# Softmax attention and hedgehog attention on one core: zero matmuls in more places, score pairs repeated, a start without DMA transposes

## The chip, the core and the metric

The kernel runs on one core of a Trainium2 chip. The core has five engines with a queue of instructions each: PE (TensorE, matmuls; PEld in the profile is its weight load), DVE (VectorE), ACT (ScalarE), POOL (GpSimd) and SP (SyncE, which here only issues DMAs). PE writes its results to PSUM, which has eight banks of 128 partitions by 512 floats; DVE and ACT read them there. An engine works through its own queue in order, and semaphores hold an instruction back until another engine or a DMA has done what it needs. The metric is the time on the device in microseconds (us).

PE's array can be used whole (128 rows by 128 columns), as four row tiles (32 rows each, four small contractions side by side) or as four column tiles (four narrow outputs side by side). The profile shows beside every stretch which share of its full clock PE was granted ("PEclk", 1.00 or 0.50 at any one moment).

## What is computed

Two layers of attention over 2048 tokens of width 512, with 32 heads of width 16, in bfloat16; their outputs are put side by side.

```
A:  q, k, v = split(x @ wqkv)
    p = softmax(q @ k.T * 16**-0.5)          # per head, 2048 x 2048
    out_A = (p @ v) @ wo
B:  q, k, v = split(x @ wqkv)
    phi(t) = concat(softmax(t @ w_phi), softmax(-(t @ w_phi)))
    kv = phi(k).T @ v ;  z = sum(phi(k))     # per head, 32 x 16
    out_B = (phi(q) @ kv / (phi(q) @ z + 1e-6)) @ wo
out = concat(out_A, out_B)
```

Layer A is nearly all of the work: 32 x 2048 x 2048 scores, each needed once for the row maximum and once for the exponential.

## The kernel before

**The plan.** The program isn't written in the order in which it runs. While it is built, a planner in Python steps through an imagined time. Every operation is a node with an engine, what it depends on, a booked duration and a priority; at each step `try_eng` (ACT, DVE, POOL, SP) or `try_pe` (PE) picks what starts next. The order that comes out is written into the engines' queues, and the chip keeps that order whatever its own times are. Bookings are simple sums: a 512-column matmul 0.213 us, an activation columns / 1200 + 0.067, a DVE instruction columns / 960 + 0.07.

**Layer A by units.** A unit is four heads (one head group of eight; each head lies on 32 partitions of its own) by 512 queries. There are 8 x 4 of them; the first and the last are cut into four of 128 queries, which makes 38. For a unit:

1. `try_m1_of` (L758): scores, queries by keys, one 32-row tile and 512 keys each. Two go to two neighbouring banks, and one DVE instruction (L766) takes both maxima. 1024 such pairs make up nearly all of DVE's work. A pair is split into two single ones where no two banks are free (it never was in this program).
2. `row_max` (L787 to L804): DVE joins the partial maxima; POOL splits the negated maximum into two bfloat16 halves; SP transposes them by DMA and puts them in two spare rows of the unit's queries. The keys have ones there, so the next product has the maximum subtracted already.
3. `try_m2` (L831): scores again, keys by queries, one row tile per bank; ACT takes the exponential into a ring of 16 slots (L327, pT). 2048 such blocks make up nearly all of ACT's work.
4. `try_pv` (L888): four column tiles multiply the exponentials with the values; bank VB = 7 gathers a unit's 16 key blocks. The values have a column of ones, which gives the sum.
5. `normalise` (L924 to L938): ACT copies the bank out (X); DMAs, ACT and POOL multiply by the reciprocal sum; then the output projection follows as a job.

The first step runs ahead of the third; the distance is called the lead here, in units of 512 queries.

**Jobs.** All whole-array work is put in jobs with a bank of their own: the projections of A (L433 for queries and keys, L472 for values), of B (L522, L536, L582), B's small products (L590, L616) and the output projections (L632, L645). A job is cut into pieces; a piece starts when `hurts` says that DVE will not be made to wait by more than a limit (JL), which grows with the job's delay. A job's piece is booked at 0.43 us. Evacuations of jobs are ACT's.

**Layer B** is released tile by tile (`fm`, every 31.5 us of planned time) and runs between the units: DVE L547 and L549, the wide work on POOL and ACT. Its denominator is inverted on ACT as a logarithm and an exponential (den_t).

**Zero matmuls.** `try_fill` comes last in `try_pe`. A list, `area`, holds how much of the array was planned busy in the last 3.4 us. While that is under FILL = 0.46 of it, and `hurts` allows it, a matmul with zeros as moving operand is put in, which adds nothing to what it accumulates on. In row mode with a unit open in bank 7 it is one row tile (L1048); in column mode, four column tiles of 17 columns (L1059); with no unit open, a full one to a free bank (L1069). Between the units, in row mode, there is none.

**The start.** ACT's queue loads the three weight blocks of A (L403). SP's queue loads x with DMA transposes, four for every 512 tokens (L409). The first projections wait for the first four.

Of the kernel before, what the change touches and what calls it, by code (L numbers as in the profile page):

```python
# [95 lines left out]
class _Node:  # L96
    __slots__ = ("eng", "run", "deps", "occ", "lat", "prio", "at", "seq", "tok", "start", "done", "frees", "ready",
                 "after")

    def __init__(self, eng, run, deps, occ, lat, prio, at, seq):  # L100
        self.eng = eng
        self.run = run
        self.deps = deps
        self.occ = occ
        self.lat = lat
        self.prio = prio
        self.at = at
        self.seq = seq
        self.tok = None
        self.start = None  # L110
        self.done = None
        self.frees = ()
        self.ready = None
        self.after = None

# [24 lines left out]
def bass_concat_heads__softmax_full_mha__linear_kernel_hedgehog__prompt_kernel(  # L140
# [23 lines left out]
    with contextlib.ExitStack() as es:  # L164
# [20 lines left out]
        eps_t = sb("eps_t", [128, 1], F32)  # L185
# [19 lines left out]
        W3 = sb("W3", [128, 4, 16], BF)  # L205
        hmask = sb("hmask", [128, 8], F32)
# [118 lines left out]
        def act(out_, in_, func, cols, reads=(), writes=(), deps=(), prio=5, sbuf=False, at=0.0, **kw):  # L325
            c = cols / 1200.0
            return mk("act", lambda ds: P.op("act", lambda e: e.activation(out_(), in_(), func, **kw), ds),  # L327
                      reads, writes, deps, occ=c + (0.093 if sbuf else 0.067) + (0.093 if "bias" in kw else 0.0),
                      lat=c + (0.28 if sbuf else 0.26) + (0.093 if "bias" in kw else 0.0), prio=prio, at=at)
# [13 lines left out]

        jobs = []
# [14 lines left out]
        def quads(fn, n=4, size=2):  # L359
# [30 lines left out]
        pool(lambda e: e.memset(eps_t[:], 1e-6), 0.1, (), ["eps"], prio=5)  # L390
# [11 lines left out]
        for i in range(3):  # L402
            dma("wa%d" % i, lambda e, i=i: e.dma_start(  # L403
                wA[:, :, i * 512:(i + 1) * 512], wa_v[:, :, i * 512:(i + 1) * 512]), (), [("wA", i)], prio=0,
                us=0.5, land=5.5 + i, q="act")

        def load_xa(c):
            for ct in range(4):
                dma("xa%d" % c, lambda e, ct=ct: e.dma_start_transpose(  # L409
                    xAT[:, ct, c * 512:(c + 1) * 512], A_x[0][c * 512:(c + 1) * 512, ct * 128:(ct + 1) * 128]),  # L410
                    (), [("xA", c, ct)], prio=0.5 + 0.1 * c if c else 0, us=1.29, land=3.6)

        for c in range(NC):
            load_xa(c)

# [12 lines left out]
        def proj_kq(kind, G, c, want, direct):  # L428
# [6 lines left out]
                want, [("wA", 0 if kind == "q" else 1)] + [("xA", c, ct) for ct in range(4)])  # L435
# [43 lines left out]

        proj_kq("k", 0, 0, 0, True)  # L480
# [39 lines left out]
        for x in (1, 0):  # L520
            for ct in range(4):
# [3 lines left out]
                    [("wT", i) for i in range(8)] + [("BD", t) for t in range(4)])  # L525
# [63 lines left out]
        def kv_job(burst, hf, want):  # L589
# [5 lines left out]
                [("phi", k) for k in range(4)] + [("vB", k) for k in range(4)], projs)  # L595
# [14 lines left out]
        def q_side(st, want):  # L610
# [4 lines left out]
            for hf in range(2):  # L615
# [3 lines left out]
                    [("phiT", i), ("kvd", hf)])  # L619
# [40 lines left out]
        m1_of = {}  # L660
        m2 = {"u": 0, "b": 0, "n": 0, "left": []}
# [67 lines left out]
        def try_m1_of(u, sm, single):  # L729
# [13 lines left out]
            if half is not None or not pair_free() or held["m"] > 2:  # L743
# [26 lines left out]
            r1_nodes.setdefault(u, []).append(d)  # L770
            if not sm["left"] and sm["half"] is None:
# [39 lines left out]
        def try_m2():  # L811
# [7 lines left out]
            if nfree() < 1 or held["e"] >= (EMAX - 1 if held["g"] or job_ready(now) else EMAX):  # L819
# [180 lines left out]
        def try_job():  # L1000
# [6 lines left out]
            if j is None:  # L1007
                if held["g"] >= 1 or (nfree() < 1):
# [25 lines left out]

        def try_fill():
            now = state["now"]
            while area and area[0][0] < now - 3.4:
                area.pop(0)
            if "end" in state or not vz[0]:
                return False  # L1040
            low = now < 9.0 or sum(a for _, a in area) < FILL * 3.4
            if not low:
                return False
            if state["mode"] == "row" and pv["open"]:
                for r in range(4):
                    old = state["fillrow"]
                    if prow[r] <= now + 1e-6 and (old is None or old[0] == r or done_by(old[1], now)):
                        n = pe_op([lambda e, r=r: e.matmul(  # L1048
                            PS[:, VB, :], ones_t[32 * r:32 * r + 32, :], zmv[32 * r:32 * r + 32, :], start=False,
                            stop=False, tile_position=(32 * r, 0), skip_group_check=True)],  # L1050
                            [t_zmv, t_ones] + ([old[1]] if old is not None and old[0] != r else []), "row", (r,))
# [4 lines left out]
            if pv["open"]:  # L1056
                if state["mode"] == "full" or not pe_ok("col", slack=0.0):
                    return False
                pe_op([lambda e, q=q: e.matmul(  # L1059
                    PS[32 * q:32 * q + 17, VB, :], ones_t[:, 0:17], zmv[:, :], start=False, stop=False,  # L1060
                    tile_position=(0, 32 * q)) for q in range(4)], [t_zmv, t_ones], "col")
            else:
                if not pe_ok("full", slack=0.0):
                    return False
                ok = [b for b, t in bank_free.items() if t is not None and t <= now + 1e-6]
                if not ok:
                    return False
                b = ok[-1]
                pe_op([lambda e: e.matmul(PS[:, b, :], ones_t[:, :], zmv[:, :], start=True, stop=True)],  # L1069
# [196 lines left out]
```

## Time and profile before

| | |
|---|---|
| three runs | 1660.59, 1691.67, 1699.48 us; median 1691.67 |
| the profiled execution | 1687.07 us, its span 1685.3 us |
| granted PE clock, mean | 0.69 |
| DVE | 1243.9 us busy, of it L766 1202.2 us (1024 instructions) |
| ACT | 1247.1 us busy, of it exponentials 1106.8 us (2048) |
| PE | 1605.2 us busy (10027 matmuls in the trace), of it zero matmuls L1048 860.6 us |
| POOL | 368.5 us busy |
| first and last score reduce | start at 18.9 and 1577.4 us |

Durations of matmuls that run side by side on several tiles overlap; a line's busy time is the time in which at least one runs that is put down to it. A row of a group reads: line, engine, operation, what it writes and reads, shapes, count; busy us and mean ns of one; idle time of the engine ahead of them and what ended it. Counts of a program's order, used below, are of the instructions as they stand in the queues, which hold no time.

### The profile page before, as it was taken

To read this page: it belongs to the slowest core of one execution; us is meant where nothing else is said; L and a number is where in the kernel's file an instruction comes from. 1 tells how busy PE (TensorE), PEld (TensorE's weight loads), DVE (VectorE), ACT (ScalarE), POOL (GpSimd) and SP (SyncE) were. 2 spreads that over 40 slices of the span, in tenths; PEclk is the share of its full clock that TensorE was granted. 3 is DMA by queue.
4 is the path that set the end of the run, shared out by engine and by line. 5 is a ranking of instruction groups with operands and counts; after the bars stand their busy time and mean duration, and the time that the engine had idled before them with its cause. 6 is when DMAs were issued, how large, how long until landed. Compare 5 with 4: busy or idle time off the path is not lost.

```text
span 1685.3 us, 24949 instructions
## 1 busy us (share of the span) xinstructions
PE 1605.2 (95%) x10027; PEld 471.6 (28%) x10085; DVE 1243.9 (74%) x1129; ACT 1247.1 (74%) x2475; POOL 368.5 (22%) x502
## 2 busy tenths in 40 slices
PE   5888999999999999999999999999999999999998
PEld 1332332222222322222222222222222222222234
DVE  5999996888799976798888666667788666666300
ACT  2887986788778966788778666667777666666666
POOL 2193731322222321132222122122210000000000
PEclk9997995777688955588777555556668555555557
DMA  5201000000001001111111011001100000000000
GB/s 114 55 5 40 5 6 5 5 6 5 4 15 9 5 1 18 18 24 18 21 30 21 11 17 15 14 11 18 24 16 22 5 4 5 4 3 7 6 4 17
DMA packets 70509, 26.71 MB, mean 16 GB/s; under 512 B 60728, under 2 KB 68472, under 8 KB 70392
## 3 DMA queue, kind: packets, MB, share of 16 engines
q1 hardware_dynamic: 68664, 23.47, 9.7%
q10 hardware_dynamic: 1728, 1.64, 0.3%
q8 instruction: 79, 1.29, 0.3%
q14 instruction: 38, 0.31, 0.1%
HBM read 3.16 MB, written 4.19 MB: 4 GB/s over the span
## 4 chain that ended last, share of the span: by engine, by line
PE 66%; DVE 19%; ACT 10%; POOL 3%; issue 1%; DMA 1%; SPq 0%; ACTq 0%; DVEq 0%; POOLq 0%
PE PS L1048 22%; DVE part L766 17%; PE PS L831 17%; PE PS L758 10%; PE PS L888 10%; ACT pT L327 8%; PE PS L536 2%; POOL QT L463 2%; PE PS L645 2%; PE PS L632 1%; PE PS L433 1%; PE PS L472 1%; DVE mB L547 1%; DVE mB L549 1%; ACT KT L327 0%
## 5 line engine op out<-in xcount | busy, mean ns | idle before, releaser
L766 DVE TENSOR_REDUCE part<-PS 128x2 f32<-128x1024 f32 x1024 | 1202.2, 1219 | 315.8 <-PE PS L1048 134.0
L327 ACT ACTIVATE pT<-PS 128x512 bf16<-128x512 f32 x2048 | 1106.8, 626 | 322.5 <-PE PS L831 153.1
L1048 PE MATMUL PS<-zmv,ones_t 32*128 32x512 bf16 x2176 | 860.6, 522 | 0.3
L831 PE MATMUL PS<-QT,KT 32*128 32x512 bf16 (+1 forms) x2432 | 769.0, 456 | 13.8 <-ACT pT L327 4.7
L758 PE MATMUL PS<-KT,QT 32*128 32x512 bf16 x2048 | 613.2, 500 | 20.0 <-DVE part L766 17.9
L1048 PEld LDWEIGHTS PS<-zmv,ones_t 32*128 32x128 bf16 x2176 | 223.1, 114 | 227.9 <-issue 187.2
L831 PEld LDWEIGHTS PS<-QT,KT 32*128 32x128 bf16 x2432 | 176.8, 100 | 369.6 <-ACT pT L327 236.0
L888 PE MATMUL PS<-pT,VP 128*17 128x512 bf16 (+1 forms) x2432 | 262.8, 452 | 0.4
L758 PEld LDWEIGHTS PS<-KT,QT 32*128 32x128 bf16 x2048 | 116.5, 99 | 174.5 <-DVE part L766 104.2
L888 PEld LDWEIGHTS PS<-pT,VP 128*17 128x17 bf16 x2432 | 55.4, 91 | 278.1 <-issue 265.8
L551 POOL TENSOR_TENSOR uB<-pB,mB 128x512 f32<-128x512 f32 x32 | 33.8, 1057 | 378.9 <-DVE mB L547 342.5
L938 POOL TENSOR_TENSOR QT<-X,Yd 128x256 bf16<-128x256 f32 (+1 forms) x67 | 45.5, 696 | 244.9 <-ACT pT L327 88.6
L796 POOL TENSOR_SCALAR stage<-mrow 128x16 bf16<-128x16 f32 (+1 forms) x38 | 9.3, 246 | 365.1 <-DVE mrow L787 365.1
L568 POOL TENSOR_TENSOR wA<-eB,rB 128x1024 bf16<-128x1024 bf16 x32 | 61.7, 1927 | 72.1 <-ACT rB L327 65.6
L976 DVE TENSOR_TENSOR QT<-PS,Yd 128x128 bf16<-128x128 f32 x1 | 0.3, 293 | 100.5 <-ACT Yd L327 100.5
L433 PE MATMUL PS<-xAT,wA 128*128 128x512 bf16 x118 | 33.8, 396 | 21.1 <-DMA xAT<-in_A_x_dram 9.8
L536 PE MATMUL PS<-Wf,xBT 128*128 128x512 bf16 x115 | 47.8, 525 | 4.2 <-issue 2.5
L557 POOL TENSOR_TENSOR sB<-eB 128x512 f32<-128x512 bf16 x32 | 36.9, 1153 | 49.9 <-ACT eB L327 49.9
L626 POOL TENSOR_TENSOR oB<-yB,den_t 128x512 bf16<-128x512 f32 x16 | 16.9, 1054 | 125.6 <-ACT den_t L327 125.6
L463 POOL TENSOR_SCALAR QT<-SG,kmask 128x512 bf16<-128x512 bf16 x28 | 43.2, 1562 | 0.6 <-ACT SG L327 0.6
L645 PE MATMUL PS<-WOp,QT 128*128 128x512 bf16 x113 | 36.0, 443 | 2.8 <-issue 1.2
L560 POOL TENSOR_TENSOR sB<-sB 128x256 f32<-128x256 f32 x64 | 36.0, 562 | 4.2
(83 smaller groups left out, 520.2 us busy)
## 6 DMA issues: line engine op xcount, KB each, us to landing
Yd<-Yd SPq DMA_DIRECT2D x120, 32.0 KB, 3.2
out_dram<-xAT SPq DMA_DIRECT2D x16, 128.0 KB, 1.7
out_dram<-OA SPq DMA_DIRECT2D x15, 128.0 KB, 1.7
wA<-in_A_wqkv_dram ACTq DMA_DIRECT2D x3, 512.0 KB, 5.8
QT<-mcols SPq DMA_DIRECT2D x60, 4.0 KB
mcols<-stage SPq DMA_TRANSPOSE x38, 2.3
WOp<-in_A_wo_dram SPq DMA_DIRECT2D x8, 64.0 KB, 3.1
woB<-in_B_wo_dram SPq DMA_DIRECT2D x1, 512.0 KB, 3.8
```

The source lines that it names most:

```text
L327: return mk("act", lambda ds: P.op("act", lambda e: e.activation(out_(), in_(), func, **kw), ds), reads, writes, deps, occ=c + (0.093 if s ...
L433: j = job(quads(lambda e, b, ct: e.matmul(PS[:, b, :], wA[:, ct, col:col + 128], xAT[:, ct, sl], start=(ct == 0), stop=(ct == 3))), want, ...
L463: kq_nodes[(kind, g, c)] = pool(lambda e, g=g, gl=gl: e.tensor_scalar(T[:, g, sl], SG[:, k, :], kmask[:, gl:gl + 1], None, ALU.mult), 0.7, ...
L536: j = job(quads(lambda e, b, ct: e.matmul(PS[:, b, :], xBT[:, ct, st * 128:(st + 1) * 128], Wf[:, x, ct, :], start=(ct == 0), stop=(ct == ...
L568: pool(lambda e: e.tensor_tensor(phiB[k].rearrange("p (g f) -> p g f", f=16), e3, rB[:, i, :].unsqueeze(2).broadcast_to([128, 64, 16]), AL ...
L645: j = job(quads(lambda e, b, i: e.matmul(PS[:, b, :], QT[:, i, st * 128:(st + 1) * 128], WOp[:, i, :], start=(i == 0), stop=(i == 7)), 8), ...
L758: fns = [lambda e, rr=rows[i], b=banks[i]: e.matmul(PS[:, b, :], QT[32 * rr:32 * rr + 32, g, q0 + 128 * qt:q0 + 128 * qt + 128], KT[32 * r ...
L766: d = dve(lambda e: e.tensor_reduce(part[:, ub, off + m:off + m + k], PS[:, banks[0]:banks[-1] + 1, :], AX.X, ALU.max), 512 * k, (), (), d ...
L831: fns = [lambda e, kt=kg * ns + j, j=j: e.matmul(PS[:, bank, j * nq:(j + 1) * nq], KT[32 * r:32 * r + 32, g, kt * 128:(kt + 1) * 128], QT[ ...
L888: fns.append(lambda e, r=r, s=s, kt=kt, j=j: e.matmul(PS[32 * r:32 * r + 17, VB, 0:nq], VP[:, kt, 8 * (g // 2) + 2 * r + g % 2, :], pT[:, ...
L938: mul_nodes[u] = pool(lambda e, a=a: e.tensor_tensor(QT[:, g, q0 + a:q0 + a + w], X[:, ub, a:a + w], Yd[:, ub, a:a + w], ALU.mult), w * 0. ...
L1048: n = pe_op([lambda e, r=r: e.matmul(PS[:, VB, :], ones_t[32 * r:32 * r + 32, :], zmv[32 * r:32 * r + 32, :], start=False, stop=False, til ...
```

## The change

- **Zero matmuls** (`try_fill`). They may now be put in between two units as well, once the unit before is copied out of bank 7 (then each starts and ends its own accumulation there). In row mode a row tile is put in while the planned area is under FILL + FROW, and no longer asks `hurts`; where the lack is larger and `hurts` is small, a group of four column tiles is put in instead (32 columns each); in full mode a full one. What a column or full one may cost by `hurts` grows with the lack (FC + FS x lack). The window is 3.3 us and FILL 0.44.
- **Score pairs repeated** (`again`). In row mode, while area is lacking, the last score pair is computed a second time into the same banks, if its reduce hasn't started and DVE is planned busy for long enough. The reduce then waits for the repeat.
- **The start.** The first 512 rows of x come as they are, by two loads into the buffer SG; 16 matmuls with an identity transpose them, and DVE and ACT copy them out by halves. Two small weight blocks for the first head pair are loaded first on ACT's queue, the rest on SP's.
- **Bookings.** A job has the width of its columns (at least 128), so that short projections are booked short; `job_len` gives `hurts` the piece's own length. JL is 0.05 in place of 0.15.
- **The lead.** `lead()` tells it. Over LB = 1.7, with jobs ready, the score phase keeps to three banks and single instructions; the exponentials' limit of banks looks at the lead too. Over 1.5, or after the last score, DVE may take a plain evacuation that waits for ACT.
- **B's denominator** is inverted on POOL, with an addition and a power of -1, in place of ACT's two.
- Before the first reduce, a job may hold up to four banks.

```diff
-        eps_t = sb("eps_t", [128, 1], F32)
+        cons = sb("cons", [128, 64], F32)
...
+            if func is ACT.Copy and not kw:
+                n.alt = (lambda ds: P.op("dve", lambda e: e.tensor_copy(out_(), in_()), ds), cols / 960.0 + 0.07,
+                         cols / 960.0 + 0.24)
...
-        def job(pieces, want, reads=(), deps=(), rel=0.0):
+        def job(pieces, want, reads=(), deps=(), rel=0.0, cols=512):
             n = mk("pe", None, reads, (), deps, at=rel, queue=False)
             j = _Job(n, pieces, want)
+            j.width = max(cols, 128) / 2400.0
...
-        for i in range(3):
-            dma("wa%d" % i, lambda e, i=i: e.dma_start(
-                wA[:, :, i * 512:(i + 1) * 512], wa_v[:, :, i * 512:(i + 1) * 512]), (), [("wA", i)], prio=0,
-                us=0.5, land=5.5 + i, q="act")
+        for h in range(2):
+            dma("xn%d" % h, lambda e, h=h: e.dma_start(
+                SG[:, 2 * h:2 * h + 2, :], A_x[0][256 * h:256 * h + 256, :].rearrange("(t p) n -> p t n", p=128)), (),
+                [("SG", 2 * h), ("SG", 2 * h + 1)], prio=0, us=0.45, land=3.0)
+        load_w("wk0", ("wA", 1, 0), 512, 640, 3.4, "act", 0)
+        load_w("wq0", ("wA", 0, 0), 0, 128, 3.8, "act", 0)
+        for i, (lo, key) in enumerate(((1024, ("wA", 2)), (640, ("wA", 1)), (128, ("wA", 0)))):
+            load_w("wa%d" % i, key, lo, lo + (512 if lo == 1024 else 384), 6.0, "sp", 0.65)
...
-        for c in range(NC):
+        for c in range(1, NC):
             load_xa(c)
...
+        for ct in range(4):
+            j = job(quads(lambda e, b, t, ct=ct: e.matmul(
+                PS[:, b, t * 128:(t + 1) * 128], SG[:, t, ct * 128:(ct + 1) * 128], ident[:],
+                start=True, stop=True), 4, 4), -10 + ct, ["ident"] + [("SG", t) for t in range(4)], cols=128)
+            projs.append(j.node)
+            fn = (lambda ct=ct: xAT[:, ct, 0:512], lambda j=j: PS[:, j.bank, :])
+            if ct % 2:
+                evac(j, dve(lambda e, fn=fn: e.tensor_copy(fn[0](), fn[1]()), 512, (), [("xA", 0, ct)], prio=0))
+            else:
+                evac(j, act(fn[0], fn[1], ACT.Copy, 512, (), [("xA", 0, ct)], prio=0))
...
-            act(lambda: den_t[:, :], lambda: y3[:, :, 16], ACT.Ln, 32, [("yB", 0), ("yB", 1), "eps"], ["den"],
-                prio=BP, sbuf=True, bias=eps_t[:, 0:1])
-            act(lambda: den_t[:, :], lambda: den_t[:, :], ACT.Exp, 32, ["den"], ["den"], prio=BP, sbuf=True,
-                scale=-1.0)
+            pool(lambda e: e.tensor_tensor(den_t[:, :], y3[:, :, 16], cons[:, 32:64], ALU.add), 0.25,
+                 [("yB", 0), ("yB", 1), "cons"], ["den"])
+            pool(lambda e: e.tensor_tensor(den_t[:, :], den_t[:, :], cons[:, 0:32], ALU.pow), 1.5,
+                 ["cons"], ["den"])
...
-            if held["m"] >= 4 or nf < 1:
+            tight = lead() > LB and (held["g"] > 0 or job_ready(now))
+            if held["m"] >= (3 if tight else 4) or nf < 1:
                 return False
             k = 2
+            single = single or tight
...
-            if nfree() < 1 or held["e"] >= (EMAX - 1 if held["g"] or job_ready(now) else EMAX):
+            if nfree() < 1 or held["e"] >= (
+                    EMAX - 1 if lead() <= LB and (held["g"] or job_ready(now)) else EMAX):
...
+        def again():
+            if last["m1"] is None:
+                return False
+            fns, rows, n, d = last["m1"]
+            now = state["now"]
+            if d.start is not None or not pe_ok("row", rows, 0.0):
+                return False
+            if max(free["dve"], n.done) < now + 0.213 + 0.26 + 0.08:
+                return False
+            k = pe_op(fns, [], "row", rows)
+            n.tok, n.done = k.tok, k.done
+            d.ready = None
+            fills[0] += 0.5
+            return True
...
-            low = now < 9.0 or sum(a for _, a in area) < FILL * 3.4
-            if not low:
-                return False
-            if state["mode"] == "row" and pv["open"]:
+            lack = 1.0 if now < 9.0 else FILL - sum(a for _, a in area) / 3.3
+            mode = state["mode"]
+            if lack > -FDUP and mode == "row" and again():
+                return True
+            opened = pv["open"]
+            vdeps = [t_zmv, t_ones]
+            if not opened:
+                if pv["u"] >= NU:
+                    return False
+                if pv["u"] > 0:
+                    x = xev_nodes.get(pv["u"] - 1)
+                    if x is None or not done_by(x, now):
+                        return False
+                    vdeps.append(x)
+            kw = dict(start=not opened, stop=not opened, skip_group_check=True)
+            if mode == "row" and lack > -FROW and not (lack > LCOL and hurts(0.213) <= FC):
...
+            if lack <= 0 or mode == "row" and lack < LACK:
+                return False
+            if hurts(0.213) > FC + FS * lack:
+                return False
...
-                    PS[32 * q:32 * q + 17, VB, :], ones_t[:, 0:17], zmv[:, :], start=False, stop=False,
-                    tile_position=(0, 32 * q)) for q in range(4)], [t_zmv, t_ones], "col")
+                    PS[32 * q:32 * q + 32, VB, :], ones_t[:, 0:32], zmv[:, :],
+                    tile_position=(0, 32 * q), **kw) for q in range(4)], vdeps, "col")
...
-        FILL = 0.46
+        FILL = 0.44
+        FROW = 0.1
+        LB = 1.7
+        LEAD = 1.5
+        FDUP = 0.0
+        LCOL = 0.03
+        LACK = 0.02
+        FC = 0.03
+        FS = 3
         WA = 0
-        JL = 0.15
+        JL = 0.05
...
-            if hurts(0.43) <= JL + job_late(now) and try_job():
+            if hurts(job_len()) <= JL + job_late(now) and try_job():
                 return True
-            return hurts(0.22) <= 0.03 and try_fill()
+            return try_fill()
...
+            if k == "dve" and (m1["u"] >= NU or lead() > LEAD):
+                for n in waiting["act"]:
+                    if n.alt is not None:
+                        w = n.when()
+                        if w is not None and w <= now + 1e-6 and (best is None or best.prio > 0):
+                            best = n
+                            break
```

More of the change, by code (lines that the diff above doesn't have):

```diff
@@ L114, in __init__ @@
         self.after = None
+        self.alt = None
     def when(self):
@@ L1048, in try_fill @@
                         n = pe_op([lambda e, r=r: e.matmul(
[L1049 to L1051 removed]
+                            PS[:, VB, :], ones_t[32 * r:32 * r + 32, :], zmv[32 * r:32 * r + 32, :],
+                            tile_position=(32 * r, 0), **kw)],
+                            vdeps + ([old[1]] if old is not None and old[0] != r else []), "row", (r,))
                         state["fillrow"] = (r, n)
@@ L1161, in late_job, with lead @@
             return False
+        def lead():
+            a = sum(units[u][3] / 512.0 for u in range(m1["u"]))
+            if m1["u"] in m1_of:
+                a += m1_of[m1["u"]]["m"] / 64.0
+            b = sum(units[u][3] / 512.0 for u in range(m2["u"])) + m2["b"] / 64.0
+            return a - b
         def try_eng(k):
@@ L1171, in try_eng @@
                     best = n
+            if k == "dve" and (m1["u"] >= NU or lead() > LEAD):
[5 more added lines that the diff above has]
+                            break
+                if best is not None and best.eng == "act":
+                    waiting["act"].remove(best)
+                    best.eng = "dve"
+                    best.run, best.occ, best.lat = best.alt
+                    waiting["dve"].append(best)
             if best is None:
```

64 lines of the change are left out of this document (40 added, 24 removed).

## The prediction

> **What bounds the kernel now.** I read the page first: shares, then the forty slices.
>
> ```profile
> span 1685.3 us, 24949 instructions
> PE 1605.2 (95%) x10027; PEld 471.6 (28%) x10085; DVE 1243.9 (74%) x1129; ACT 1247.1 (74%) x2475; POOL 368.5 (22%) x502
> PE   5888999999999999999999999999999999999998
> DVE  5999996888799976798888666667788666666300
> PEclk9997995777688955588777555556668555555557
> ```
>
> PE looks like the bound at 95%, but the DVE line follows PEclk: where PEclk is 9, DVE is 9; where PEclk is 5, DVE is 6. A slice is 42 us. So I asked for the busy time of each engine in stretches that are wholly on one side. The columns are the stretch, its length, then PE, PEld, DVE, ACT and POOL busy with instruction counts, and the granted clock.
>
> ```profile
> 548.00:595.70 47.70, 45.42 (x372) 15.71 (x369) 47.70 (x45) 45.77 (x95) 17.34 (x22) 1.00 0.06 5
> 476.30:537.50 61.20, 58.34 (x442) 18.70 (x440) 60.88 (x57) 58.03 (x119) 15.26 (x19) 1.00 0.08 13
> 18.90:148.50 129.60, 109.25 (x1064) 39.78 (x1079) 123.83 (x115) 96.88 (x187) 62.37 (x70) 1.00 0.20 45
> 906.40:1165.70 259.30, 256.29 (x1219) 64.13 (x1225) 176.05 (x157) 173.42 (x340) 48.21 (x64) 0.50 0.10 15
> 1305.70:1558.90 253.20, 252.36 (x1267) 66.36 (x1267) 163.46 (x141) 170.37 (x317) 11.13 (x28) 0.50 0.06 5
> ```
>
> At clock 1.00, DVE is the bound (47.70 of 47.70): 238.5 us hold 45 + 57 + 115 = 217 DVE instructions, **1.099 us each**. At clock 0.50, PE is the bound (252.36 of 253.20): 512.5 us hold 298, **1.720 us each**. Two limits, and the clock says which holds. Next: what makes the clock fall? The matmuls of a warm and a cold stretch (548.0 to 595.7, then 1305.7 to 1558.9), grouped by line:
>
> ```profile
> L1048 PE MATMUL PS<-zmv,ones_t 32*128 32x512 bf16 x101 | 27.5, 377 | 0.0
> L831 PE MATMUL PS<-QT,KT 32*128 32x512 bf16 x80 | 26.5, 383 | 0.9 <-ACT vB L327 0.7
> L758 PE MATMUL PS<-KT,QT 32*128 32x512 bf16 x80 | 16.8, 383 | 1.1 <-DVE part L766 1.0
> L888 PE MATMUL PS<-pT,VP 128*17 128x512 bf16 x84 | 8.3, 385 | 0.0
> L582 PE MATMUL PS<-wA,xBT 128*128 128x512 bf16 x8 | 2.1, 382 | 0.0
> L590 PE MATMUL PS<-vB,wA 128*128 128x68 bf16 x16 | 0.9, 195 | 0.0
> L536 PE MATMUL PS<-Wf,xBT 128*128 128x512 bf16 x3 | 0.8, 379 | 0.2 <-issue 0.2
> ```
> ```profile
> L1048 PE MATMUL PS<-zmv,ones_t 32*128 32x512 bf16 x391 | 190.1, 622 | 0.3
> L831 PE MATMUL PS<-QT,KT 32*128 32x512 bf16 x304 | 126.2, 613 | 0.7 <-ACT pT L327 0.7
> L758 PE MATMUL PS<-KT,QT 32*128 32x512 bf16 x268 | 111.3, 615 | 0.0
> L888 PE MATMUL PS<-pT,VP 128*17 128x512 bf16 x304 | 46.1, 596 | 0.0
> ```
>
> I count area: a matmul that uses a quarter of the array (a row tile of 32, or one of four column tiles) counts a quarter of its columns, at 0.213 us for 512 columns at full clock (L888 shows it: 385 ns warm, 596 cold; halving the clock adds one streaming time, 0.211). Warm: 345 quarters and 12 fulls (the 16 short ones count 2) give 18.4 + 2.8 us, 0.44 of 47.7. Cold: 1267 quarters, 67.6 us, 0.27 of 253.2, with PE never idle. So the clock follows streamed area, not busy time.
>
> The threshold comes from the windows in which the clock changes. All changes lie on a grid of 3.41 us. The first and the last of the 22 windows that ended in a fall before the tail, then the first and the last of the 22 cold stretches behind them:
>
> ```profile
> 145.15:148.56 3.41, 1.33 (x14) 0.56 (x14) 1.81 (x3) 1.16 (x4) 0.00 (x0) 1.00 0.17 38
> 1302.27:1305.68 3.41, 3.10 (x21) 0.94 (x18) 3.41 (x4) 3.41 (x9) 0.00 (x0) 1.00 0.00 0
> 148.56:172.46 23.90, 23.56 (x111) 5.97 (x114) 20.67 (x19) 16.57 (x34) 0.96 (x1) 0.50 0.11 7
> 1305.68:1664.08 358.40, 355.81 (x1960) 102.68 (x1964) 177.15 (x154) 240.26 (x450) 15.67 (x39) 0.50 0.06 5
> ```
>
> Their area is 0.22 and 0.30. Over the 182 warm windows, a limit of 0.365 puts 3 on the wrong side; if the zero matmuls are left out of the count, the best limit is wrong on 21. So zeros count. The same 0.365, in full-clock columns, splits cold windows that rise from those that don't (9 wrong of 306). Cold, PE must therefore be 73% filled to get out, and the packing of four row queues seldom does it: the 22 stretches last 47.5 us on average (1044.5 us in all).
>
> The Trainium skill, "TensorE: Matmul & The Clock Gate", section "Why this matters for your kernels", asks for "No PE-idle gaps >~3µs between matmul bursts" and says idling is what drops the clock. The cold stretch above, 252.36 busy of 253.20 at 0.50, disagrees; taken by that rule the fills would buy nothing, which is the first rival's time.
>
> **The change, part by part.** The program's order gives counts. Per 32x512 or column tile, a zero matmul is one instruction. Before: 2176 row zeros, 52 column zeros, 17 full. After: 2768, 532 and 26, and 174 repeated score matmuls (87 pairs). Total area goes from 582.8 to 652.1 us at full clock. What matters is where it lies. Take as ruler three successive pair reduces (L766), 3.6 us of DVE time: before, 170 of 1021 such windows have area under 0.36; after, 9. Over four reduces it is 152 against 0. So nearly all planned holes are gone.
>
> *Body at full clock.* Where the start and the first and last reduce lie, then the DVE work of the whole run:
>
> ```profile
> 0.79 21.22 SPq L409 DMA_TRANSPOSE xAT<-in_A_x_dram  x15
> 0.83 1.57 ACTq L403 DMA_DIRECT2D wA<-in_A_wqkv_dram  x3
> 11.75 1.86 PE L433 MATMUL PS<-xAT,wA 128*128 128x512 bf16 x4 [9.85 <-DMA xAT<-in_A_x_dram]
> 18.89 3.49 DVE L766 TENSOR_REDUCE part<-PS 128x2 f32<-128x1024 f32 x3
> ...
> 1577.41 1.23 DVE L766 TENSOR_REDUCE part<-PS 128x2 f32<-128x1024 f32 x1 [1.30 <-PE PS L1048]
> ```
> ```profile
> L766 DVE TENSOR_REDUCE part<-PS 128x2 f32<-128x1024 f32 x1024 | 1202.2, 1219 | 315.8 <-PE PS L1048 134.0 <-PE PS L758 113.9 <-PE PS L831 64.1
> L547 DVE TENSOR_REDUCE mB<-pB 128x32 f32<-128x512 f32 x32 | 21.7, 678 | 1.9 <-ACT pB L327 1.9
> L549 DVE TENSOR_REDUCE mB<-pB 128x32 f32<-128x512 f32 x32 | 21.6, 676 | 0.0
> L787 DVE TENSOR_REDUCE mrow<-part 128x16 f32<-128x64 f32 (+1 forms) x38 | 9.0, 238 | 0.0
> L443 DVE TENSOR_SCALAR QT<-PS,kmask 128x512 bf16<-128x512 f32 x2 | 1.5, 751 | 17.5 <-PE PS L433 17.4
> ```
>
> 1024 + 64 + 38 = 1126 instructions, all warm, take 1126 x 1.099 = 1237 us. Now they take 1560 (18.9 to 1578.9, first and last reduce), which by the two rates means 519 cold ones. Nine pairs are split into single reduces (two of 0.68 for one of 1.22: +1 us), and eight evacuations before the last reduce move to DVE (as L443, 0.75: +6 us, with ACT relieved). Body: **1245**, that is 1133 at the warm rate.
>
> *Start.* The first four DMA transposes become two plain loads, 16 short matmuls and four copies. But in the new order, PE takes the projection of key block 1 ahead of the first score matmul, and it waits for block 1's DMA transposes. These are four on SP behind two loads, so they land about when the first four landed before, 1 us later (12.7), then 4 matmuls and the first pair: first reduce at **15** instead of 18.9. Bounds 11 (no such wait) and 19. Three weight loads go from ACT's queue to SP's, between the transposes of block 1 and those of blocks 2 and 3, which start 1.6 us later by the L403 row; each block gives 8 pair reduces (9 us) and takes 4 x 1.41 us to issue, so DVE doesn't run dry.
>
> *Tail.* After the last reduce the order leaves 75 exp blocks instead of 117, because the score phase is held to a lead of about 1.6 units instead of 2.2.
>
> ```profile
> L327 ACT ACTIVATE pT<-PS 128x512 bf16<-128x512 f32 x117 | 64.8, 602 | 27.8 <-PE PS L831 18.2 <-PE PS L1048 9.6
> 379.41 13.72 ACT pT L327 x28
> 1673.49 3.54 ACT L327 ACTIVATE pT<-PS 128x512 bf16<-128x512 f32 x7
> ```
>
> Now 106.4 us for 117. Back to back an exp takes 13.72 / 28 = 0.49: 75 x 0.49 = 37, some 6 of other ACT work, and 8 from the last exp (1677.0) to the end: **51**; at the present cold pace 68.
>
> *Waits on the fills.* Row fills no longer ask whom they delay, and a repeat holds its reduce back. The nearest row is DVE's waiting, 505 to 590, nearly all warm:
>
> ```profile
> DVE part L766 <- PE PS L1048: 2.5, 3, 1.1
> ```
>
> 2.5 of 85 us over 1245 us is 37 us for 2245 fills; with 3500 it is 58, so **+22**. Lower bound 0; upper 592 + 174 + 120 more slots of 0.213 all on the path, 190.
>
> *Falls that remain.* The order says 170 of 1021 where the trace fell in 22 of 182, so 0.73 of what the order says. 9 of 1021 gives 0.6% of 371 windows, 2.4; I take **3**, since a wait the plan doesn't know (the 145.15 window, PE busy 1.33) can recur. Cold, PE bounds, and its area is up 12%: 1.720 x 652.1 / 582.8 = 1.925 us an instruction. A stretch of 47.5 us then loses 47.5 x (1 - 1.099 / 1.925) = 20 us. Three: **+61**.
>
> *At nothing.* The denominator's Ln and Exp go from ACT to two POOL operations, 32 in all. POOL is busy 22%; at its slowest row,
>
> ```profile
> L568 POOL TENSOR_TENSOR wA<-eB,rB 128x1024 bf16<-128x1024 bf16 x32 | 61.7, 1927 | 72.1 <-ACT rB L327 65.6
> ```
>
> they would fill 62 us in which POOL is otherwise idle. A power operation is in no row; only past about 19 us (half a unit, what a lead of 1.6 leaves the row maximum's hop over POOL and SP) would it delay the exps. Jobs booked short only let the plan place them tighter; PE at full clock has the room.
>
> Sum: 15 + 1245 + 51 + 22 + 61 = 1394, and the profiled execution lay 1.8 over its span (1687.07): **1396**. That execution is 0.3% under the median of the three runs, 1691.67, which span 1660.59 to 1699.48; 2% is about what can be told from no change.
>
> **Rivals.** *The fills are only work (slower).* If the clock keeps to busy time or to something the fills don't touch, the same 519 instructions run cold, at 1.925: 614 x 1.099 + 519 x 1.925 = 1674, with 15, 22, a cold tail of 68 and 2: 1781. It decides from 455 cold instructions on (1720). For it: cold stretches in which PE is full of zeros (391 of 1267) and stays cold. Against: 21 wrong windows when zeros are left out. 0.08. In between, 373 to 455 cold, within 2%: 0.04.
>
> *Unplanned waits keep cooling it.* The plan's times drift from the chip's, windows planned at 0.44 dip, and a third of the body is cold: one instruction in 1 / (0.667 / 1.099 + 0.333 / 1.925) = 1.282, 1133 x 1.282 = 1453, in all 1543. For it: the 145.15 window; a higher area makes the cold state slower to leave. Against: exps back to back run at the rate the plan books. 0.14.
>
> *ACT becomes the bound.* Warm it is busy 45.77 of 47.70, and with a short lead DVE waits for it. 1247 at 96% is 1299, and its late start (18.9, and 33 idle of the 129.6 to 148.5) makes 1351: inside the forecast, not a separate time.
>
> **How the numbers follow.** Forecast, few falls: 0.70 (1310 to 1480). Cooling by waits: 0.14. Same: 0.04. Slower: 0.08. No falls and no fill waits, under 1310: 0.04. Range 1310 to 1560: the floor is the sum without fills' waits and falls, 1313; the top takes in the third-cold case. Faster by over 2%: 0.70 + 0.14 + 0.04 = 0.88.
>
> **What would show it.** PEclk nearly all 9, with isolated dips of under 50 us; mean clock above 0.9; DVE 9 until the tail; first reduce near 15 us; about 75 exps behind the last reduce in some 50 us; L1116's share in DVE's waits under 60 us. It would be wrong if stretches of hundreds of us at 0.50 remain, if DVE has gaps at clock 1.00 (fills in the way), or if POOL's power operation runs for tens of us.

## The result and the profile after

The changed kernel took 1505.8 us in the median of its four runs (1468.61, 1469.92, 1541.68, 1645.61), the kernel before 1683.88: a ratio of 0.8807, 95% interval 0.863 to 0.8983. The interval is worked out from the two fastest of the four, because the other two ran at a mean clock of 0.826 and 0.761 against 0.870 in the profiled execution (1469.92 us, span 1468.2).

The page of the kernel after, with the lines that answer to those shown of before:

```profile
span 1468.2 us, 27515 instructions
PE 1405.9 (96%) x11290; PEld 486.4 (33%) x11356; DVE 1232.7 (84%) x1153; ACT 1205.1 (82%) x2432; POOL 461.7 (31%) x538
PE   8998999999999999999999999889999999999998
DVE  7998999999999999655867868886697599999960
PEclk9999999999999999555856759985697599999999
```

The first sixteen slices and the last eight are at full clock, but for two short stretches (10 us from 139.71 on, 3 us from 1238.80 on), and DVE is at 8 or 9 there except in the first slice and the tail. Between them, from 587 to 1174 us, the old picture is back: long stretches at half clock. The stretches of one clock, in the same columns as before (stretch, length, PE, PEld, DVE, ACT, POOL busy with counts, granted clock):

```profile
12.90:136.30 123.40, 114.27 (x1139) 41.79 (x1156) 121.45 (x112) 91.54 (x178) 57.39 (x67) 1.00 0.19 38
149.95:583.45 433.50, 423.52 (x3679) 155.95 (x3696) 432.35 (x417) 414.54 (x856) 146.65 (x185) 1.00 0.08 8
586.86:709.74 122.88, 122.21 (x586) 30.70 (x585) 72.58 (x64) 75.32 (x139) 30.89 (x30) 0.50 0.09 13
740.46:795.07 54.61, 54.28 (x262) 13.47 (x257) 33.35 (x30) 32.95 (x62) 15.42 (x15) 0.50 0.10 14
982.81:1054.48 71.67, 67.83 (x327) 16.11 (x330) 42.07 (x37) 40.37 (x76) 16.67 (x19) 0.50 0.09 15
1242.20:1418.70 176.50, 176.13 (x1588) 71.33 (x1583) 175.51 (x161) 173.19 (x357) 11.82 (x31) 1.00 0.09 8
1418.90:1468.20 49.30, 43.40 (x785) 22.98 (x785) 2.55 (x6) 39.82 (x87) 3.43 (x8) 0.99 0.11 19
```

Warm, a DVE instruction takes 733.4 / 690 = 1.063 us (1.099 before); cold, 249.16 / 131 = 1.90 (1.720 before). Nine cold stretches lie ahead of the tail. What starts them is in the list of what PE waited for (us in all, times, longest), whose first two lines are:

```profile
PE PS L668 <- DMA xAT<-oB: 19.6, 8, 4.0
PE PS L618 <- DMA wA<-in_B_wqkv_dram: 4.5, 1, 4.5
```

L668 is B's output projection. In the kernel before, the same projection (L632) never waited for oB's transpose. The groups of the page say why it comes late now:

```profile
L660 POOL TENSOR_TENSOR den_t<-den_t,cons 128x32 f32<-128x32 f32 x16 | 87.3, 5457 | 1.2
```

L660 is the power of -1 on POOL: 5.46 us for 32 columns, booked in the plan at 1.5. The first fall inside the bad stretch, along the timelines of POOL, SP and PE:

```profile
576.31 5.46 POOL L660 TENSOR_TENSOR den_t<-den_t,cons 128x32 f32<-128x32 f32 x1
581.85 1.06 POOL L662 TENSOR_TENSOR oB<-yB,den_t 128x512 bf16<-128x512 f32 x1
582.93 1.20 SPq L666 DMA_TRANSPOSE xAT<-oB  x1
585.62 0.38 PE L668 MATMUL PS<-woB,xAT 128*128 128x512 bf16 x1 [1.90 <-DMA xAT<-oB]
586.71 0.49 PE L872 MATMUL PS<-QT,KT 32*128 32x512 bf16 x1 [0.71 <-ACT pT L329]
```

The power takes 4 us more than planned, so the product, its transpose on SP and the projection come as much later. PE keeps its written order and stands still at L668 for 1.9 us, then again for 0.71. At the next grid point, 586.86, the clock falls, for 122.88 us. Six more of the nine falls (740.46, 829.21, 914.54, 948.67, 982.81, 1238.80) lie in such a wait, or at most 1.2 us behind its end (start, length, then the wait in brackets):

```profile
739.33 0.81 PE L668 MATMUL PS<-woB,xAT 128*128 128x512 bf16 x3 [2.17 <-DMA xAT<-oB]
829.69 1.89 PE L668 MATMUL PS<-woB,xAT 128*128 128x512 bf16 x4 [1.83 <-DMA xAT<-oB]
913.57 0.81 PE L668 MATMUL PS<-woB,xAT 128*128 128x512 bf16 x3 [2.67 <-DMA xAT<-oB]
950.16 1.49 PE L668 MATMUL PS<-woB,xAT 128*128 128x512 bf16 x3 [3.53 <-DMA xAT<-oB]
985.98 0.63 PE L668 MATMUL PS<-woB,xAT 128*128 128x512 bf16 x1 [4.04 <-DMA xAT<-oB]
1238.84 0.63 PE L668 MATMUL PS<-woB,xAT 128*128 128x512 bf16 x1 [2.69 <-DMA xAT<-oB]
```

The fall at 1119.34 comes by another queue. The transpose L666 stands on SP until the late oB is there, and behind it stands L965, which has nothing to do with layer B: it fetches a unit's sums (lr) out of X, which ACT had copied by 1112.06. ACT waits for lr, and PE for ACT's next exponential:

```profile
1114.75 1.19 SPq L666 DMA_TRANSPOSE xAT<-oB  x1
1115.98 0.57 SPq L965 DMA_DIRECT2D lr<-X  x1
1117.74 0.26 ACT L329 ACTIVATE lr<-lr 32x64 f32<-32x64 f32 x1 [2.87 <-DMA lr<-X]
1118.52 0.39 PE L872 MATMUL PS<-QT,KT 32*128 32x512 bf16 x1 [2.88 <-ACT pT L329]
```

The fall at 139.71 comes with L618's 4.5 us. So each of the nine falls has one of the nine waits of PE over 1.2 us that lie between 20 us and the last reduce, and eight of these come from the late oB. The eighth wait at L668, 0.77 us at 1083, brought no fall.

### The profile page after: what moved, and what is told of

Read it like the earlier page. It is cut to its first block, busy times and chain, and to the rows that moved or that the text cites. A ratio compares the mean times of both kernels' runs of the same rounds, so it can differ in the third digit from the quotient of the medians.

```text
span 1468.2 us, 27515 instructions
## 1 busy us (share of the span) xinstructions
PE 1405.9 (96%) x11290; PEld 486.4 (33%) x11356; DVE 1232.7 (84%) x1153; ACT 1205.1 (82%) x2432; POOL 461.7 (31%) x538
## 4 chain that ended last, share of the span: by engine, by line
PE 57%; DVE 25%; POOL 6%; ACT 6%; DMA 3%; issue 1%; SPq 0%; POOLq 0%; ACTq 0%; DVEq 0%
DVE part L805 24%; PE PS L1116 18%; PE PS L872 15%; PE PS L797 9%; PE PS L929 7%; ACT pT L329 5%; POOL den_t L660 3%; POOL QT L489 2%; PE PS L572 2%; PE PS L1130 2%; PE PS L668 1%; DMA xAT<-oB 1%; PE PS L498 1%; POOL oB L662 1%; DVE mB L585 1%
## 5 line engine op out<-in xcount | busy, mean ns | idle before, releaser
L805 DVE TENSOR_REDUCE part<-PS 128x2 f32<-128x1024 f32 (+1 forms) x1033 | 1184.1, 1209 | 175.5 <-PE PS L797 73.1
L329 ACT ACTIVATE pT<-PS 128x512 bf16<-128x512 f32 x2048 | 1075.7, 615 | 163.8 <-PE PS L872 64.9
L1116 PE MATMUL PS<-zmv,ones_t 32*128 32x512 bf16 x2768 | 854.7, 420 | 0.7
L872 PE MATMUL PS<-QT,KT 32*128 32x512 bf16 (+1 forms) x2432 | 694.8, 381 | 8.3 <-ACT pT L329 3.8
L797 PE MATMUL PS<-KT,QT 32*128 32x512 bf16 x2222 | 525.3, 421 | 8.1 <-DVE part L805 4.5
L1116 PEld LDWEIGHTS PS<-zmv,ones_t 32*128 32x128 bf16 x2768 | 246.6, 99 | 167.4 <-issue 81.2
L929 PE MATMUL PS<-pT,VP 128*17 128x512 bf16 (+1 forms) x2432 | 221.0, 381 | 0.3
L660 POOL TENSOR_TENSOR den_t<-den_t,cons 128x32 f32<-128x32 f32 x16 | 87.3, 5457 | 1.2
L658 POOL TENSOR_TENSOR den_t<-yB,cons 128x32 f32<-128x32 f32 x16 | 4.2, 263 | 153.5 <-ACT yB L329 137.1
L1130 PE MATMUL PS<-zmv,ones_t 128*32 128x512 bf16 x532 | 47.9, 410 | 0.4
L668 PE MATMUL PS<-woB,xAT 128*128 128x512 bf16 x51 | 22.7, 539 | 21.6 <-DMA xAT<-oB 19.6
L572 PE MATMUL PS<-Wf,xBT 128*128 128x512 bf16 x110 | 39.4, 458 | 3.2 <-issue 1.8
```

The source lines that it names most:

```text
L329: n = mk("act", lambda ds: P.op("act", lambda e: e.activation(out_(), in_(), func, **kw), ds), reads, writes, deps, occ=c + (0.093 if sbuf ...
L572: j = job(quads(lambda e, b, ct: e.matmul(PS[:, b, :], xBT[:, ct, st * 128:(st + 1) * 128], Wf[:, x, ct, :], start=(ct == 0), stop=(ct == ...
L660: pool(lambda e: e.tensor_tensor(den_t[:, :], den_t[:, :], cons[:, 0:32], ALU.pow), 1.5, ["cons"], ["den"])
L797: fns = [lambda e, rr=rows[i], b=banks[i]: e.matmul(PS[:, b, :], QT[32 * rr:32 * rr + 32, g, q0 + 128 * qt:q0 + 128 * qt + 128], KT[32 * r ...
L805: d = dve(lambda e: e.tensor_reduce(part[:, ub, off + m:off + m + k], PS[:, banks[0]:banks[-1] + 1, :], AX.X, ALU.max), 512 * k, (), (), d ...
L872: fns = [lambda e, kt=kg * ns + j, j=j: e.matmul(PS[:, bank, j * nq:(j + 1) * nq], KT[32 * r:32 * r + 32, g, kt * 128:(kt + 1) * 128], QT[ ...
```

## The experiments

All are against the kernel before on the same chip. Where a number of windows is given, it is counted in the program's order as in the prediction. "Clock" is the mean of the profiled execution.

**The power operation booked at what it takes.**

```diff
-            pool(lambda e: e.tensor_tensor(den_t[:, :], den_t[:, :], cons[:, 0:32], ALU.pow), 1.5,
+            pool(lambda e: e.tensor_tensor(den_t[:, :], den_t[:, :], cons[:, 0:32], ALU.pow), 5.4,
```

> The changed kernel with one number altered: POOL's power operation is booked at 5.4 us instead of 1.5 (its row in the trace of after: 5.457 us). Theory (the late denominator makes PE wait at L668 for oB's transpose, that hole lets the clock fall, and the cold stretches between 586 and 1174 us are its cost): no wait of PE at L668 over 0.5 us, at most 3 cold stretches instead of 9, mean clock over 0.95, 1290 to 1340 us. Rival (the holes come from anywhere the plan is thin, the power operation only happens to lie there): cold stretches and time as in after, 1450 to 1500 us.

1297.7 us (1286.77 to 1307.9), ratio 0.7754 (0.7667 to 0.7841). The page and the list of PE's waits:

```profile
span 1285.0 us, 27528 instructions
DVE  7999799999999999999999999999999999999950
ACT  3778799999999999999999999999999899999997
...
PE PS L618 <- DMA wA<-in_B_wqkv_dram: 4.4, 1, 4.4
...
PE PS L668 <- DMA xAT<-oB: 0.5, 1, 0.5
```

One cold stretch is left ahead of the tail, 137 to 148 us, behind L618's wait; the clock is 0.996. POOL does the same work for as long (460.8 us busy). One number in the planner, and 183 us of span are gone, some 23 for each of the eight cold stretches that are missing. ACT's two waits for lr (2.68 us at 585.92, 2.87 at 1117.74) are gone as well. The power operation's lateness was the cost, not its length. The stretches of this run are at the warm rate throughout:

```profile
12.90:137.30 124.40, 114.48 (x1138) 41.81 (x1156) 121.81 (x113) 91.27 (x178) 59.77 (x69) 1.00 0.20 39
147.60:600.00 452.40, 442.10 (x3837) 161.60 (x3860) 451.14 (x436) 432.53 (x896) 155.00 (x197) 1.00 0.09 9
600.00:1236.00 636.00, 626.12 (x5447) 233.25 (x5464) 634.09 (x597) 607.15 (x1260) 230.09 (x234) 1.00 0.15 20
```

1212.8 us for 1146 instructions, 1.058 each. Here the kernel is bound by DVE from end to end, with ACT right behind (607.15 of 636.00).

**The denominator back on ACT.**

```diff
-            pool(lambda e: e.tensor_tensor(den_t[:, :], y3[:, :, 16], cons[:, 32:64], ALU.add), 0.25, ...
-            pool(lambda e: e.tensor_tensor(den_t[:, :], den_t[:, :], cons[:, 0:32], ALU.pow), 1.5, ...
+            act(lambda: den_t[:, :], lambda: y3[:, :, 16], ACT.Ln, 32, ..., bias=cons[:, 32:33])
+            act(lambda: den_t[:, :], lambda: den_t[:, :], ACT.Exp, 32, ..., scale=-1.0)
```

> The changed kernel with B's denominator back on ACT as logarithm and exponential; all else as in after. Theory of the late denominator: as with the right booking, 1290 to 1340 us, ACT busy some 9 us more than in after; if the power operation's 87 us on POOL matter beyond their lateness, this one is faster than the one with the right booking. Rival (holes from anywhere): 1450 to 1500 us.

1290.51 us (1290.33 to 1318.93), ratio 0.7773 (0.7714 to 0.7832): the same as with the right booking. PE waits nowhere for oB's transpose in this run either. So POOL's 87 us cost nothing by themselves, and what the move to POOL takes off ACT brings next to nothing (the shortest runs are 1290.33 here and 1286.77 with the right booking). The profiled execution is the longest of the four, 1318.93: it has a second cold stretch, 543.92 to 612.19, behind a window in which PE waits for no input and streams 0.37 of the array. The plan alone can be thin enough.

**The old zero matmuls in the new kernel.** With the power booked at 5.4, `try_fill` and its call as before, FILL 0.46.

> As the one with the power operation booked at 5.4 us, but the zero matmuls by the rules of before (none between units in row mode, no repeats, 17 columns, always asking what they delay). Its order has 90 of 1021 three-reduce windows under 0.36, after 9, before 170. Theory (the fills keep the clock): falls come back, some 12 cold stretches or more, clock 0.75 to 0.85, 1450 to 1600 us. Rival (start, lead and short bookings brought the gain): under 1350 us.

1646.65 us (1603.62 to 1670.65), clock 0.714, sixteen cold stretches ahead of the tail. With the old zeros, all of the start, the lead and the bookings together are worth some 40 us of the 390 between 1687 and 1298 (by the medians; its runs spread over 67). The miss: 1647 lies over the 1450 to 1600 that the theory gave, and the clock under its 0.75.

**The new zero matmuls and repeats in the old kernel.**

> The kernel before with the new zero matmuls and repeats alone; start, lead, bookings and denominator as before. Its order has 94 of 1021 windows under 0.36. Theory (fills bring the clock only together with the shorter lead and bookings that let them in): 1450 to 1600 us. Rival (fills alone do it all): under 1380 us, that is the all-warm time of 1270 plus 6 for the start, 25 for a tail of 117 exps and a few falls.

1501.49 us (1472.86 to 1507.87), clock 0.843. Fills alone bring half of the way, some 186 us; with the 40 of the rest that is far from 390, so each needs the other. The order's 94 thin windows show that the fills aren't let in everywhere when the rest of the plan is the old one; PE's waits for inputs are few, the longest being

```profile
PE PS L582 <- DMA wA<-in_B_wqkv_dram: 6.8, 1, 6.8
```

once. Yet there are 18 cold stretches ahead of the tail. One (15.08) belongs to the start, one (144.78) begins in that wait; the others come from thin plans rather than from late inputs. That follows from the counts: each of the 17 falls behind the first reduce follows a window with 0.37 of the array or less, but no run took the thin windows away one by one.

**No repeats.** `FDUP = -9`, the power booked at 5.4.

> As the one with the power operation booked at 5.4 us, with no score pair repeated; the plan puts in 148 more column zeros and 30 fewer row zeros in their place. 14 of 1021 windows under 0.36. Theory (area is area, whoever streams it): 1285 to 1320 us, at most 3 cold stretches. Rival (repeats fill holes that nothing else can): 5 falls or more, over 1340 us.

1297.24 us (1285.03 to 1307.45), against 1297.7 with repeats. The repeats of the change do nothing that column zeros don't do.

**No zero matmul between units.** `if not opened and now > 20.0: return False`, the power booked at 5.4.

> As the one with the power operation booked at 5.4 us, but no zero matmul between units after the start (while bank 7 isn't opened by a unit), as before the change in row mode. 30 of 1021 windows under 0.36, 10 of 1020 over four reduces. Theory (each unit's border then has a thin place): 4 to 10 cold stretches, 1330 to 1430 us. Rival (the borders don't matter, the higher level inside the units does it): 1285 to 1310 us.

1339.8 us (1333.33 to 1384.91), ratio 0.8003 (0.7927 to 0.8079); six cold stretches, 119 us in all, the last two near the end (1216 to 1308). 42 us of the gain hang on the borders of the units.

**The planned level at the limit.** FILL 0.36, FROW 0, the power booked at 5.4.

> As the one with the power operation booked at 5.4 us, with FILL 0.36 in place of 0.44 and FROW 0 in place of 0.1: all new rules, but the planned level lies at the limit read from the traces (0.36). Area 564 us at full clock in place of 652; 252 of 1021 windows under 0.36. Theory (a limit at 0.36 of the array in 3.41 us): cold for over a third of the time, 1480 to 1700 us. Rival (a limit further down, or no limit on area): under 1350 us, and less waiting on PE.

1488.19 us (1456.59 to 1505.51), clock 0.719, 24 cold stretches. The limit is where the traces had put it. Over this run's windows, the 159 warm ones that stayed have an area of 0.37 or more, the 25 that fell 0.37 or less. Unexpected is the time: the clock is hardly better than before's 0.69, yet it is 195 us shorter than before's. Three of its cold stretches:

```profile
618.27:696.77 78.50, 77.98 (x433) 16.90 (x429) 62.27 (x55) 60.10 (x122) 29.20 (x27) 0.50 0.12 17
887.92:963.01 75.09, 74.53 (x406) 15.60 (x405) 59.98 (x54) 57.57 (x116) 26.19 (x22) 0.50 0.10 16
1280.45:1352.13 71.68, 70.60 (x415) 15.30 (x412) 57.95 (x51) 57.11 (x113) 2.85 (x8) 0.50 0.06 5
```

225.3 us for 160 DVE instructions: 1.41 each, not 1.72 or 1.90. Cold, PE is the bound, and zeros are work on it. That asked for the last two experiments of this section.

**No limit on the lead.** LB and LEAD 99, the power booked at 5.4.

> As the one with the power operation booked at 5.4 us, with no limit on the lead (LB and LEAD 99). 11 of 1021 windows under 0.36. Theory (the lead only sets how many exps are left for the tail, at 0.49 us each, and which engine copies): 15 to 30 us longer than with the limit, 1300 to 1335 us. Rival (the short lead also feeds PE evenly, and without it windows thin out): 4 cold stretches or more, over 1350 us.

1292.36 us (1290.99 to 1292.81), ratio 0.7731 (0.7685 to 0.7777). The 15 to 30 us are a miss: the tail is longer, but the body ends sooner, with DVE's last maximum at 1230.77 (1235.97 with the limit) and the end at 1291.1 (1285.0). The lead is worth 6 us of the profiled spans, and nothing in the medians (1297.7 with the limit). Its four runs are the closest together of all.

**B's weights booked later.** Landing after 11 us for the value weights and 8 for the others, the power booked at 5.4.

> As the one with the power operation booked at 5.4 us, and B's value weights booked to land after 11 us instead of 5.5, B's other weights after 8 instead of 3.6. Theory (the one cold stretch left, 137 to 148 us, follows a wait of 4.4 us at L618 for these weights): no cold stretch before the tail, 1275 to 1300 us, a narrower spread. Rival (L618 waits for something the booking doesn't move): the stretch stays, time as with the power booking alone, 1298.

1305.88 us (1291.81 to 1359.18): no gain, and no narrower. L618's wait is gone, but another operation takes its place,

```profile
PE PS L558 <- DMA wA<-in_B_wqkv_dram: 2.3, 1, 2.3
```

and in the middle of that wait, at 149.30, the clock falls until 176.61. Booking one arrival later moved the wait to the next reader of the same loads.

**No zeros at all, in the new kernel and in the old.** `... or now > 20.0: return False` in `try_fill`; the new one with the power booked at 5.4.

> As the one with the power operation booked at 5.4 us, with no zero matmul and no repeat after the first 20 us: 468 us of area at full clock in place of 652. Theory (in the cold state zeros are work on the engine that bounds: cold stretches took 1.91 us per DVE instruction in after and 1.41 with the low level): cold for over 80% of the time, yet 1380 to 1530 us, faster than the 1647 with the old zeros. Rival (what counts is the clock alone): 1650 us or more.

1492.37 us (1490.75 to 1492.92), ratio 0.8987 (0.8915 to 0.9059).

> The kernel before with no zero matmul after the first 20 us: 461 us of area in place of 583. Theory (before's zeros kept the clock up 38% of the time but made the cold 62% longer by more): 1430 to 1600 us, faster than before. Rival (they paid for themselves): over 1700 us.

1499.95 us (1497.33 to 1503.33), ratio 0.9041 (0.8945 to 0.9137). The page of the old kernel without zeros, then one stretch of it:

```profile
PE   5898999999999999999999999999999999999988
DVE  4997988889889998988898988888998799888800
PEclk9997655555558655555555855555555575555556
...
600.00:1000.00 400.00, 379.69 (x1930) 86.17 (x1929) 353.53 (x321) 334.78 (x693) 105.07 (x135) 0.58 0.13 19
```

Cold for most of its time (clock 0.612), and still 1.25 us a DVE instruction, with DVE busy 88%. So before's zeros, which raised the mean clock to 0.69, made the kernel 190 us slower than none. And the change as it was made, 1505.8 in the median and 1468.61 at its shortest, is at most 2% faster than no zeros at all.

## Why the prediction was right, and where it was not

**What bounds the kernel: right.** Two bounds, DVE at full clock and PE at half. The limit of 0.365 of the array in 3.41 us holds in the new trace: any limit between 0.36 and 0.38 splits its 313 warm windows without an error, and 0.365 puts 2 of 112 cold ones wrong.

**Start: 15 forecast, 12.88 measured.** PE does take key block 1's projection ahead of the first score matmul, but it doesn't wait for it: three zero matmuls stand in front of it, and it starts without idle time at 11.49. The transposes had landed by then, where the forecast had 12.7.

```profile
11.49 1.03 PE L459 MATMUL PS<-xAT,wA 128*128 128x512 bf16 x3
12.88 8.10 DVE L805 TENSOR_REDUCE part<-PS 128x2 f32<-128x1024 f32 x7 [0.30 <-PE PS L797]
```

**Body at full clock: right, a little dear.** 1.099 us an instruction was forecast, 1.063 measured.

**Waits on the fills: +22 forecast, next to nothing measured.** DVE's waits from 149.95 to 583.4:

```profile
DVE part L805 <- PE PS L797: 0.3, 1, 0.3
DVE part L805 <- PE PS L1116: 0.3, 2, 0.2
DVE part L805 <- PE PS L872: 0.3, 1, 0.3
```

0.9 us in 433. The 2.5 us that it was scaled from lay wholly in a cold stretch, 537.68 to 547.92, though 505 to 590 was called nearly all warm. At half clock PE is the bound, and waiting on a zero is part of that. The sign named for this term was missed by a little: over the whole run L1116 stands for 61.0 us of DVE's waits, not under 60.

**Tail: 51 forecast, 49.3 measured**, with 73 exps. The shorter lead isn't much of a gain, though: without the limit, the body is 5 us shorter.

**Falls that remain: 3 forecast, 9 measured. This is where the 74 to 110 us between the forecast of 1396 and the result (1469.92 profiled, 1505.8 median) come from.** The cold stretches hold 193 DVE instructions in 382 us; at the warm rate these take 205, so the falls cost some 177 us where 61 stood. The body's lower rate (1143 x 1.063 = 1215, not 1245) and the 22 of the fills take 52 of that back. So it is in part luck that the profiled time lies in the 1310 to 1480 of the favoured case; its signs, a clock above 0.9 and dips of under 50 us, failed at 0.870 and 122.88. The count of thin windows was sound: with the power booked right, one or two stretches are left. The step that failed is "At nothing". It set the power operation between the slowest POOL row, 1.9 us, and 19 us, and let that whole range cost nothing, because it looked only at who else needs POOL (the row maximum's hop). At 5.46 us it lay inside. What it left out is the other queues at the end of the chain: oB, its transpose on SP with A's own DMAs behind it, and L668 standing in PE's fixed order with everything behind it. PE lost only 19.6 us by waiting at L668; the clock lost nearly all the rest.

The price of a fall held: stretches of 382 / 9 = 42 us (47.5 forecast), 1.90 us an instruction in the longer ones (1.925), 177 / 9 = 20 us lost in each (20 forecast). So the second rival, unplanned waits that keep cooling it, given 0.14, describes what happened; its third of the body cold was 27% (382 of 1406 us), its 1543 against a median of 1505.8. The forecast case is what the kernel does once that wait is gone: 1297.7, under the range, because one short fall is left of the three then, the fills' waits aren't there, and an instruction takes 1.058 us.

**The first rival fell, but half of it was true.** Zeros do hold the clock: 1647 with the old ones, 1298 with the new. But in the cold they are only work: 1.41 us an instruction with few of them, 1.72 and 1.90 with many. The prediction used this for the price of a fall and didn't ask it of the kernel before. There the zeros had already been on the wrong side, by 190 us.

The Trainium skill's rule on idle gaps ("TensorE: Matmul & The Clock Gate", section "Why this matters for your kernels") is met from the other side in these runs: waits of 1.9 and 0.71 us in one window were enough for a fall (586.86), each under its ~3 us, and PE 122.21 busy of 122.88 did not bring the clock back.

In the working, "12 fulls" should be 13 (their 2.8 us is right), and the +22 comes to 21; neither changes the forecast.

What stays open: why two of the four runs of the changed kernel had so much more cold time. The record shows the lower clock; the runs didn't tell apart a different phase of the 3.41 us grid from other causes.

## What to carry to other kernels

Where a clock follows activity, count what a filler costs when the clock has fallen all the same. Here each zero is then work on the engine that bounds: with 22 falls the zeros cost 190 us against none, with nine they came out about even, with one they gained 195. In a kernel whose order is written by a planner, a wrong booking can cost nothing on the engine that runs the operation and much on the engines whose fixed order waits for its result: follow a new operation's result to the last queue that stands still for it, and measure its duration before booking it. An operation whose duration no row shows isn't free because its own engine is idle.

## What the runs showed of the hardware

- A power of -1 on POOL took 5.457 us for 128 x 32 values (5.438 to 5.463 in 16), where an addition of the same shape (L658) took 0.263.
- The granted clock follows the streamed area. The thirteen traces have 3384 windows of 3.41 us at full clock between the first and the last score reduce; 156 of them ended in a fall. Each matmul's columns were laid from 0.06 us after its start, 512 in 0.213 us (double at half clock), with a row or column tile as a quarter and zeros like all others. Then every window that ended in a fall has 0.375 of the array or less, and every other one 0.369 or more, except one (0.335, in the kernel before). With the quarters counted as whole, the best limit is wrong on 21 windows of the kernel before, which has 22 falls.
- The same limit, 0.37 in full-clock columns, tells the half-clock windows behind which the clock rose from the others, with 43 of 1743 wrong (150 rises).
- A low clock alone costs this kernel little: without zeros it ran at a mean clock of 0.61 in 1492 to 1500 us, only 15% over the 1298 us of the run with the right booking, whose profiled execution had 0.996.
